# One line for all transfers in a planner, and the next pair's transposes between the halves of a pair

## Chip, cores and metric

One Trainium2 chip, one core. The metric is the device time of one execution in microseconds, taken as the median of several runs. A profiled execution, from which the rows come, has its own time.

## What is computed

The reference is an attention block with normalised queries and keys, followed by a bilinear feed-forward block (FFN). Batch 8, 12 heads, 448 positions, head dimension 64; the FFN has 3584 tokens, model width 768 and inner width 1536. All is float32; the weights come as float64.

```python
q_n, k_n = (rmsnorm(q, g_q), rmsnorm(k, g_k))
scores = scale * np.matmul(q_n, k_n.transpose(0, 1, 3, 2))
scores = scores - np.max(scores, axis=-1, keepdims=True)
attn = np.exp(scores)
attn = attn / (np.sum(attn, axis=-1, keepdims=True) + 1e-09)
attn_out = np.matmul(attn, v)
x = attn_out.transpose(0, 2, 1, 3).reshape(B * S, H * D)
out = (x @ w_a) * (x @ w_b) @ w_out
```

## The kernel before

**Pairs.** Attention is done for two heads at a time: 48 pairs, six to a batch, two heads side by side on 128 partitions. For pair `p`, `loads` (L408) brings q, k and v on SP's queue into two buffers each. `normalize` (L423) squares q and k on ScalarE (L435), sums on VectorE (L442), scales the sums (L449), takes the power -0.5 on GpSimd (L453, tile `ms`), and multiplies q by it on VectorE (L457, tile `qn`); the factor of k goes into the exponential. `transposes` (L467) turns k and q on TensorE (L486, tile `pt`), and ScalarE copies both into `qkT` (L491, L493). Keys are handled in four chunks `c`: `scores` (L499) makes `sc` on TensorE (L506) and takes the exponentials on ScalarE (L512, tile `ET`, four buffers); `values` (L518) multiplies them with v into `o` (L527); the sums over keys `su` come from matmuls with ones (L562), for pairs 0 to 11 directly from `ET`, later from `sum`, which VectorE (L540) and GpSimd (L542) add up first. `sums_over_keys` then copies `su` to a tile `rec` (L581), spreads one row of it over 112 partitions by a transfer (`few<-rec`, L587), takes the reciprocal on VectorE (L598), writes it to DRAM (`inv<-few`, L591) and brings it back over all partitions (`rec<-inv`, L595). `put_out` (L609) copies `o` into a tile `x` (L620) and multiplies by `rec` (L624). Every sixth pair (`p % 12 == 11`) instead takes the reciprocal of `su` in place (L572).

**Halves.** A pair has two halves on TensorE: chain `A{p}` holds the scores of chunks 0 and 1 and the values of chunks 2 and 3 of the pair before; chain `B{p}` the scores of chunks 2 and 3, the sums, and the values of chunks 0 and 1. `sc` has two buffers, and from pair 12 on (`LEAD`) the transposes use one of them. Scores use half of the array's rows, values and sums half of its columns, transposes and FFN products all of it (`mode`).

**Weights and FFN.** The FFN of two batches at a time (`beta` 0 to 3) is done by a scheme with seven products in place of eight, for which 18 tiles of weight factors `st` are made: `factors` (L342) loads 1.5 MB of float64 words on ScalarE's queue (L364 for w_out, L367 for w_a and w_b, tiles `hraw` and `lraw`), rounds them to float32 in seven steps (L268 on ScalarE, L269 to L277 on VectorE), forms differences (L377), and writes the result to DRAM (`kept`, L385 and L388), from where later rounds read it (`stream`, L391). `GATES` says after which pair's scores a factor may begin, `seq` in which order they are made. `quarter_products` (L763) multiplies x with the factors (`pq`, L779, 21 matmuls for each of 12 factors, in groups of three), `last_product` (L668) multiplies the result with the factors of w_out (`po`, L707).

**The order.** Nothing of this is issued where it is written. Each step is an `op` with an engine, an expected time in us, a `key`, the tiles that it reads and writes, and, for transfers, kilobytes (`kb`). `Plan.run` (L70) plays the program through with these figures: of the steps of an engine that could start now it takes the one with the lowest key, and the order that comes out is the order in which each engine is given its instructions. An engine then works strictly in that order: a step whose input is late holds up all behind it. Transfers on SP's and ScalarE's queues share eight semaphore lanes; an issue also waits until the last transfer on its lane has landed. The expected landing of a transfer (L143 to L147) is kept for SP and ScalarE apart: 250 KB per us, or 200 while the other is at work, and 2.5 us on top. At the start, 12 times four matmuls (`WARM`, L868) that compute nothing keep TensorE busy. Keys are counted in pairs: a load has `p - 2`, normalisation `p - 4`, the way of the reciprocals `p - 3`.

Of the kernel before, what the change touches and what calls it, by code (L numbers as in the profile page):

```python
# [9 lines left out]
FP32 = mybir.dt.float32  # L10
# [15 lines left out]
class Plan:  # L26
# [10 lines left out]
    LANES = 8  # L37
    LAG = 0.1
# [31 lines left out]
    def run(self):  # L70
# [18 lines left out]
        opened, free, modes, cands, dma, port = {}, {}, {}, {}, {"SP": 0.0, "ACT": 0.0}, 0.0  # L89
# [21 lines left out]
        while any(cands.values()):  # L111
# [20 lines left out]
            for x in members(n):  # L132
# [35 lines left out]
def kernel(  # L168
# [40 lines left out]
    NJ = 4  # L209
# [86 lines left out]
    def fast_body(ld, wk, ps_s, ps_o, ps_mm, dram):  # L296
# [4 lines left out]
        WARM = 12  # L301
# [40 lines left out]
        def factors(n, key, early, after):  # L342
# [16 lines left out]
            for part in range(2):  # L359
# [9 lines left out]
                op("ACT", 0.45, key - 2.5, load, after, [f"{row}/{part}"], kb=768)  # L369
# [38 lines left out]
        def loads(p, nm):  # L408
# [12 lines left out]
            op("SP", 0.5 if nm != "k" else 0.9, p - (1.8 if nm == "v" else 2.0), emit, [], [t], new=[t], kb=230)  # L421

        def normalize(p):  # L423

            ms, key = tile_of(f"ms{p}", "ms", 3), p - NORM
            for s, nm in enumerate("qk"):
                sq = tile_of(f"sq{nm}{p}", "sq", 1)

                def square(nm=nm):
# [4 lines left out]
                    if p < LEAD or SQUARE == "ACT":  # L434
                        nc.scalar.activation(t, flat, AF.Square)  # L435
                    else:
                        two[SQUARE].tensor_tensor(t, flat, flat, ALU.mult)

                def reduce(nm=nm, s=s):
                    if s == 0:  # L440
                        rs[p] = wk.tile([SP, 2, 2 * NJ], FP32, tag="ms", name="ms", bufs=3)
                    nc.vector.tensor_reduce(rs[p][:, s], xs["sq", nm, p], AX, ALU.add)  # L442
                e = "ACT" if p < LEAD else SQUARE
                op(e, {"ACT": 0.65, "POOL": 1.05, "DVE": 0.7}[e], key, square, [f"{nm}{p}"], [sq], new=[sq], lock=e != "ACT")
                op("DVE", 0.69, key, reduce, [sq], [ms], new=[ms] if s == 0 else [])

            def mean():
                msf = rs[p].rearrange("p s n -> p (s n)")
                nc.vector.tensor_scalar(msf, msf, 1.0 / D, 1e-6, ALU.mult, ALU.add)  # L449

            def root():
                msf = rs[p].rearrange("p s n -> p (s n)")
                nc.gpsimd.tensor_tensor(msf, msf, expo, ALU.pow)  # L453
# [8 lines left out]
            op("DVE", 0.18, key, mean, [], [ms])  # L462
            op("POOL", 2.95, key, root, [], [ms])
            qn = tile_of(f"qn{p}", "qn", 1)
            op("DVE", 0.7, key, apply, [ms, f"q{p}"], [qn], new=[qn], lock=True)

        def transposes(p):  # L467
            qkT = tile_of(f"qkT{p}", "qkT", 2)
            key = p - 0.5 if p < LEAD else p
            for n, nm in ((1, "k"), (0, "q")):  # L470
# [23 lines left out]
                after = [] if p < LEAD else [f"scored{p - 1}"]  # L494
# [4 lines left out]
        def scores(p, c, chain):  # L499
# [14 lines left out]
            op("PE", 0.76, p, product, [f"qkT{p}/0", f"qkT{p}/1"], [sc] + ([f"scored{p}"] if c == NJ - 1 else []), new=[sc],  # L514
               mode="rows", chain=chain)
            op("ACT", 1.12, p, exps, [sc, f"ms{p}"], [E], new=[E])
# [30 lines left out]

        def sums_over_keys(p, cs, chain):
# [19 lines left out]
            if p % (2 * HP) == 2 * HP - 1:  # L568
# [28 lines left out]
            op("SP", 0.8, p - 3.0, spread_out, [t], [few], new=[few], kb=20, dmas=2)  # L597
# [455 lines left out]
```

## Time and profile before

| | us |
|---|---|
| median of three runs | 1647.89 |
| lowest and highest run | 1640.82, 1650.4 |
| profiled execution, own time | 1654.08 |
| its span | 1652.2 |
| TensorE busy | 1604.7 |
| VectorE, ScalarE, GpSimd busy | 729.3, 432.7, 401.8 |

The span runs from the first to the last instruction, and 1.9 us of the execution lie around it. A row of the timeline gives start, duration, engine, line, operation, output and input, and in brackets the idle time before it with what ended it; matmuls of one group stand together (x8), and a float32 matmul of the program shows as two records. Ends of matmuls are modelled, so the distance between starts is the safer measure.

### The profile page before, as it was taken

How to read it: one execution, taken by the hardware profiler on the slowest of the kernel's cores; microseconds unless marked ns; L12 is line 12 of the kernel's file. 1: busy time of each engine (PE TensorE's matmuls, PEld its weight loads, DVE VectorE, ACT ScalarE, POOL GpSimd, SP SyncE). 2: the span in 40 equal slices, each digit the busy share in tenths (PEclk: the TensorE clock that was granted, in tenths of full speed). 3: DMA queues.
4: the chain of work that ended last, by engine and by line, in shares of the span. 5: the costliest groups of instructions: out<-in, count | busy, mean ns of one | idle time of the engine just before them, and what ended most of it. 6: DMA issues, size and time to landing. Idle time of an engine off the chain costs nothing.

```text
span 1652.2 us, 15068 instructions
## 1 busy us (share of the span) xinstructions
PE 1604.7 (97%) x5546; PEld 786.7 (48%) x5546; DVE 729.3 (44%) x992; ACT 432.7 (26%) x777; POOL 401.8 (24%) x200
## 2 busy tenths in 40 slices
PE   7888799999999999999999999999999999999998
PEld 5333344455444455555444455555544555555554
DVE  4776657789567532222267541122235422222331
ACT  4666563311355610000255620000034000000000
POOL 3232354211366620100265630000133000100000
PEclk9999999999999999999999999999999999999999
DMA  5676325354433443212232333322222332222121
GB/s 183 229 228 219 122 68 183 100 209 149 147 97 99 117 141 123 100 67 100 80 97 85 107 104 129 109 71 96 96 68 81 110 134 100 96 71 91 70 103 50
DMA packets 131656, 191.21 MB, mean 116 GB/s; under 512 B 62196, under 2 KB 120308, under 8 KB 121844
## 3 DMA queue, kind: packets, MB, share of 16 engines
q1 hardware_dynamic: 103828, 137.06, 25.8%
q10 hardware_dynamic: 27744, 53.09, 8.9%
q8 instruction: 46, 0.75, 0.2%
q14 instruction: 38, 0.31, 0.1%
HBM read 154.01 MB, written 35.94 MB: 115 GB/s over the span
## 4 chain that ended last, share of the span: by engine, by line
PE 83%; DMA 7%; DVE 6%; issue 1%; ACT 1%; POOL 1%; SPq 1%; ACTq 0%; DVEq 0%; POOLq 0%
PE pq L779 43%; PE po L707 23%; PE sc L506 6%; PE o L527 6%; DMA inv<-few 2%; PE su L562 2%; DMA few<-rec 2%; PE pt L486 2%; DMA rec<-inv 1%; DVE x L643 1%; DMA k_sb<-in_k_dram 1%; DVE st L377 1%; POOL ms L453 1%; DVE st L277 1%; DVE su L572 1%
## 5 line engine op out<-in xcount | busy, mean ns | idle before, releaser
L779 PE MATMUL pq<-x,st 128*128 128x448 f32 x2016 | 768.3, 542 | 3.2 <-DVE t L836 3.2
L779 PEld LDWEIGHTS pq<-x,st 128*128 128x128 f32 x2016 | 381.9, 191 | 378.7 <-issue 368.3
L512 ACT ACTIVATE ET<-sc,ms 112x448 f32<-112x448 f32 x384 | 216.2, 637 | 128.4 <-PE sc L506 117.5
L707 PE MATMUL po<-st,hT 128*128 128x384 f32 x744 | 247.3, 488 | 0.0
L542 POOL TENSOR_TENSOR sum<-sum,ET 112x896 f32<-112x896 f32 x72 | 162.2, 2253 | 197.9 <-DVE sum L540 180.1
L453 POOL TENSOR_TENSOR ms<-ms,expo 112x16 f32<-112x16 f32 x48 | 152.6, 3180 | 214.7 <-DVE ms L449 203.5
L506 PE MATMUL sc<-qkT 64*112 64x448 f32 x768 | 175.1, 573 | 26.2 <-ACT ET L512 14.1
L827 POOL TENSOR_TENSOR hT<-hT,t 128x448 f32<-128x448 f32 x24 | 27.9, 1164 | 676.4 <-DVE t L825 676.4
L707 PEld LDWEIGHTS po<-st,hT 128*128 128x128 f32 x744 | 139.4, 190 | 102.2 <-issue 9.5
L527 PE MATMUL o<-ET,v_sb 112*64 112x448 f32 x768 | 168.1, 560 | 1.0 <-ACT x L620 1.0
L707 PE MATMUL po<-st,fin 128*128 128x384 f32 x432 | 145.1, 489 | 0.0
L801 ACT COPY hT<-pq 128x448 f32<-128x448 f32 x24 | 12.8, 532 | 447.0 <-PE pq L779 447.0
L506 PEld LDWEIGHTS sc<-qkT 64*112 64x112 f32 x768 | 61.2, 175 | 120.0 <-issue 79.0
L707 PEld LDWEIGHTS po<-st,fin 128*128 128x128 f32 x432 | 80.6, 190 | 59.3 <-issue 7.0
L527 PEld LDWEIGHTS o<-ET,v_sb 112*64 112x64 f32 x768 | 51.1, 140 | 106.9 <-issue 101.5
L442 DVE TENSOR_REDUCE ms<-sq 112x8 f32<-112x512 f32 x96 | 65.1, 678 | 73.5 <-ACT sq L435 69.7
L727 DVE TENSOR_TENSOR o_sb<-fin,po 128x384 f32<-128x384 f32 x56 | 31.0, 554 | 149.9 <-PE po L707 146.2
L457 DVE TENSOR_TENSOR qn<-q_sb,ms 112x512 f32<-112x512 f32 x48 | 62.6, 1304 | 22.2 <-POOL ms L453 11.2
L839 POOL TENSOR_TENSOR hT<-hT,t 128x448 f32<-128x448 f32 x48 | 58.9, 1229 | 46.7 <-DVE t L836 46.7
L804 ACT COPY t<-pq 128x448 f32<-128x448 f32 x24 | 12.8, 533 | 187.2 <-PE pq L779 187.2
L832 DVE TENSOR_TENSOR hT<-U,pq 128x448 f32<-128x448 f32 x48 | 29.8, 621 | 68.2 <-PE pq L779 68.2
L836 DVE TENSOR_TENSOR t<-U,pq 128x448 f32<-128x448 f32 x48 | 29.6, 620 | 65.0 <-PE pq L779 63.9
(70 smaller groups left out, 980.8 us busy)
## 6 DMA issues: line engine op xcount, KB each, us to landing
st<-kept SPq DMA_DIRECT2D x36, 1344.0 KB
st<-kept_o SPq DMA_DIRECT2D x28, 1152.0 KB
kept<-st ACTq DMA_DIRECT2D x12, 1344.0 KB
q_sb<-in_q_dram SPq DMA_DIRECT2D x48, 224.0 KB
k_sb<-in_k_dram SPq DMA_DIRECT2D x48, 224.0 KB
v_sb<-in_v_dram SPq DMA_DIRECT2D x48, 224.0 KB
rec<-inv SPq DMA_DIRECT2D x88, 112.0 KB
kept_o<-st ACTq DMA_DIRECT2D x6, 1344.0 KB
```

The lines of the kernel that those rows point to most:

```text
L442: nc.vector.tensor_reduce(rs[p][:, s], xs["sq", nm, p], AX, ALU.add)
L453: nc.gpsimd.tensor_tensor(msf, msf, expo, ALU.pow)
L457: nc.vector.tensor_tensor(qns[p].rearrange("p j h d -> p h j d"), xs["q", p].rearrange("p h (j d) -> p h j d", d=D), rs[p][:, 0].rearrange ...
L486: nc.tensor.transpose(t[:, j * SP:(j + 1) * SP], x[:, j].rearrange("p h d -> p (h d)"), ident[0:SP, 0:SP])
L506: nc.tensor.matmul(t[:, e, 0:S], lhsT=qkTs[p][rows, 1, c * SP:(c + 1) * SP], rhs=qkTs[p][rows, 0, :], start=True, stop=True)
L512: nc.scalar.activation(E[:, e], scs[p, c][:, e, 0:S], AF.Exp, scale=rs[p][:, 1, 2 * c + e:2 * c + e + 1])
L527: nc.tensor.matmul(os_[p][e * D:(e + 1) * D, :], lhsT=xs["v", p][:, e, c * D:(c + 1) * D], rhs=ETs[p, c][:, e], start=(c == 0), stop=(c == ...
L542: two[ADD_UP].tensor_tensor(sums[p], sums[p], ETs[p, c], ALU.add)
L562: nc.tensor.matmul(sus[p][e * D:(e + 1) * D, :], lhsT=ones, rhs=x[:, e], start=(first and n == 0), stop=(last and n == len(parts) - 1))
L707: nc.tensor.matmul(held["po"][:, 0:HALF], lhsT=a[0]()[:, c], rhs=sts[beta, 12 + place_of[f]][:, c], start=(c == 0), stop=(c == MH - 1))
L779: nc.tensor.matmul(banks[bank][:, 0:S], lhsT=sts[at][:, f, c * P:(c + 1) * P], rhs=quads[x][:, c], start=(start and c == 0), stop=(stop an ...
L839: lambda i=i, n=n, nm=nm: two[TIMES].tensor_tensor(C(i, n), C(i, n), held[nm], ALU.mult), [t], [hp[i]],
```

## The change

All of it is in what the planner is told; the operations stay the same, but for two things named below.

- Transfers run on one line in the planner, at 300 KB per us with 2.5 us on top, whichever queue issues them; a k load counts as 400 KB.
- q and k loads get the key `p - 2.5`, v `p - 2.3`; the steps of the reciprocals' way go from `p - 3` to `p`.
- From pair 12 on the transposes of pair `p` get the key `p - 1.5` and wait for chunk 1 of pair `p - 1` (`half`) instead of chunk 3 (`scored`), so that they come between that pair's halves.
- The first two factors wait for k of pair 0; the gates of the others lie mostly earlier, five instead of eight use `hraw`, and their order is another one. `WARM` goes from 12 to 4.
- In the first four pairs q and k have their own scaling step and root (two instructions of 8 columns each for one of 16); `ms` is tracked in two parts, one for q and one for k.
- The FFN products name x and not also T3 and T4 as inputs.

```diff
+    RATE, LANDING = 300.0, 2.5
...
-                    dma[e] = max(dma[e], t) + ops[x][7] / (200.0 if dma["SP" if e == "ACT" else "ACT"] > t else 250.0)
-                    end[x] = dma[e] + 2.5
+                    dma = max(dma, t) + ops[x][7] / self.RATE
+                    end[x] = dma + self.LANDING
                     sent += [end[x]] * ops[x][11]
-                    if e == "SP":
-                        dma["ACT"] = max(dma["ACT"], t) + ops[x][7] / 300.0
...
-        WARM = 12
+        WARM = 4
+        APART = 4
...
-                op("ACT", 0.45, key - 2.5, load, after, [f"{row}/{part}"], kb=768)
+                op("ACT", 0.45, key - 1.5, load, after, [f"{row}/{part}"], kb=768)
...
-            op("SP", 0.5 if nm != "k" else 0.9, p - (1.8 if nm == "v" else 2.0), emit, [], [t], new=[t], kb=230)
+            op("SP", 0.5 if nm != "k" else 0.9, p - (2.3 if nm == "v" else 2.5), emit, [], [t], new=[t], kb=230 if nm != "k" else 400)
...
+            def roots(a, b, names):
+                msf = lambda: rs[p][:, a:b].rearrange("p s n -> p (s n)")
+                op("DVE", 0.18, key, lambda: nc.vector.tensor_scalar(msf(), msf(), 1.0 / D, 1e-6, ALU.mult, ALU.add), [], names)
+                op("POOL", 1.7 if b - a == 1 else 2.95, key,
+                   lambda: nc.gpsimd.tensor_tensor(msf(), msf(), expo[:, 0:2 * NJ * (b - a)], ALU.pow), [], names)
...
+            sums(0, "q")
+            if p < APART:
+                roots(0, 1, [f"{ms}/q"])
+            sums(1, "k")
+            if p < APART:
+                roots(1, 2, [f"{ms}/k"])
+            else:
+                roots(0, 2, [f"{ms}/q", f"{ms}/k"])
...
-            key = p - 0.5 if p < LEAD else p
+            key = p - 0.5 if p < LEAD else p - 1.5
...
-                after = [] if p < LEAD else [f"scored{p - 1}"]
+                after = [] if p < LEAD else [f"half{p - 1}"]
...
-            op("SP", 0.8, p - 3.0, spread_out, [t], [few], new=[few], kb=20, dmas=2)
+            op("SP", 0.8, p - 0.0, spread_out, [t], [few], new=[few], kb=20, dmas=2)
...
-                op("PE", KH * S / 595, key, emit, [f"{st}/{(0, 0, 0, 0, 4, 5, 6)[f]}", *parts(x), *parts(T3), *parts(T4)], [nm, "ffn"], new=[nm] if start else [], mode="full")
+                op("PE", KH * S / 595, key, emit, [f"{st}/{(0, 0, 0, 0, 4, 5, 6)[f]}", *parts(x)], [nm, "ffn"], new=[nm] if start else [], mode="full")
...
-        GATES = [0, 0, 1, 2, 3, 5, 7, 9, 10] + [12] * 9
-        seq = [12, 13, 14, 15, 16, 0, 1, 2, 3, 4, 5, 6, 7, 17, 8, 9, 10, 11]
+        GATES = [0, 0, 1, 1, 1, 2, 2, 2, 2, 2, 3, 5, 6, 6, 8, 8, 9, 10]
+        seq = [13, 12, 16, 14, 15, 0, 1, 2, 3, 4, 5, 6, 7, 8, 9, 10, 17, 11]
...
-                    factors(n, x * 1.1 + 0.5, x < 8, [f"scored{p - 1}"] if p else [])
+                    factors(n, x * 1.1 + 1.5, x < 5, [f"scored{p - 1}"] if p else ["k0"])
```

What this moves, at three places. First ScalarE at the start of the program (DMA rows are weight loads; `sq` are the squares of pairs 0 and 1, `qkT` the copies of the transposes), before:

```order
L231 ACTIVATE grow_63<-const-float32-0.0 1x256
L364 DMA hraw_90<-in_moe_w_out_dram 128x1536 x4
L435 ACTIVATE sq_128<-q_sb_96 112x512
L435 ACTIVATE sq_140<-k_sb_103 112x512
L863 COPY gain_60<-pg_147 128x1
L491 COPY qkT_188<-pt_178 128x448
L435 ACTIVATE sq_190<-q_sb_160 112x512
L493 ACTIVATE qkT_188<-pt_183,gain_60 128x448
L268 ACTIVATE st_93<-hraw_90 128x1536
L435 ACTIVATE sq_204<-k_sb_162 112x512
L512 ACTIVATE ET_207<-sc_198,ms_134 112x448 x2
```

and after:

```order
L230 ACTIVATE grow_63<-const-float32-0.0 1x256
L440 ACTIVATE sq_127<-q_sb_99 112x512
L440 ACTIVATE sq_133<-k_sb_105 112x512
L364 DMA hraw_90<-in_moe_w_out_dram 128x1536 x2
L867 COPY gain_60<-pg_141 128x1
L364 DMA hraw_90<-in_moe_w_out_dram 128x1536
L440 ACTIVATE sq_149<-q_sb_123 112x512
L364 DMA hraw_90<-in_moe_w_out_dram 128x1536
L492 COPY qkT_167<-pt_155 128x448
L440 ACTIVATE sq_170<-k_sb_125 112x512
L494 ACTIVATE qkT_167<-pt_160,gain_60 128x448
```

The two squares of pair 0 have moved ahead of all weight loads; pair 1's k square (the row with k_sb_125) now stands between the two copies of pair 0.

Then SP's queue in the pairs before pair 12 (`few`, `inv` and `rec` are the three legs of the reciprocals' way), before:

```order
L587 DMA few_468<-rec_432 56x1x8 x2
L591 DMA inv1_499<-few_468 112x8
L419 DMA v_sb_524<-in_v_dram 112x2x256
L595 DMA rec_432<-inv1_499 64x448 x2
L587 DMA few_549<-rec_520 56x1x8 x2
L416 DMA k_sb_565<-in_k_dram 112x8x64
L591 DMA inv2_591<-few_549 112x8
L419 DMA v_sb_594<-in_v_dram 112x2x256
L419 DMA q_sb_599<-in_q_dram 112x2x256
L416 DMA k_sb_612<-in_k_dram 112x8x64
L595 DMA rec_520<-inv2_591 64x448 x2
L587 DMA few_623<-rec_619 56x1x8 x2
```

and after:

```order
L591 DMA few_410<-rec_385 56x1x8 x2
L419 DMA q_sb_448<-in_q_dram 112x2x256
L595 DMA inv1_452<-few_410 112x8
L419 DMA v_sb_461<-in_v_dram 112x2x256
L416 DMA k_sb_482<-in_k_dram 112x8x64
L591 DMA few_488<-rec_484 56x1x8 x2
L419 DMA q_sb_519<-in_q_dram 112x2x256
L599 DMA rec_385<-inv1_452 64x448 x2
L595 DMA inv2_551<-few_488 112x8
L419 DMA v_sb_556<-in_v_dram 112x2x256
L416 DMA k_sb_580<-in_k_dram 112x8x64
L591 DMA few_600<-rec_577 56x1x8 x2
```

Before, `inv<-few` comes right behind the `few<-rec` that it needs, or behind one k load; after, a q load, and in the second pair also the return of the pair before, stand between the two. The loads of a pair keep the order q, v, k from pair to pair.

Last TensorE in the dense part from pair 12 on, where FFN products (`pq`) fill in, before:

```order
L506 MATMUL sc<-qkT 112x448 x4
L562 MATMUL su<-sum,ones 64x448 x2
L527 MATMUL o<-ET,v_sb 64x448 x4
L486 MATMUL pt<-ident,k_sb 128x112 x4
L486 MATMUL pt<-ident,qn 128x112 x4
L779 MATMUL pq<-x,st 128x448 x3
L506 MATMUL sc<-qkT 112x448 x4
L527 MATMUL o<-ET,v_sb 64x448 x4
L779 MATMUL pq<-x,st 128x448 x3
```

and after:

```order
L507 MATMUL sc<-qkT 112x448 x4
L566 MATMUL su<-sum,ones 64x448 x2
L528 MATMUL o<-ET,v_sb 64x448 x4
L507 MATMUL sc<-qkT 112x448 x4
L528 MATMUL o<-ET,v_sb 64x448 x4
L487 MATMUL pt<-ident,k_sb 128x112 x4
L487 MATMUL pt<-ident,qn 128x112 x4
L783 MATMUL pq<-x,st 128x448 x3
```

Before, the second half of a pair (with `su`) is followed by the transposes of the next, then FFN products, then that pair's first half, then FFN products. After, a second half is followed at once by the first half of the next pair, and transposes and one group of FFN products come behind that.

More of the change, by code (lines that the diff above doesn't have):

```diff
@@ L88, in run @@
         ready = {n: 0.0 for n in need}
-        opened, free, modes, cands, dma, port = {}, {}, {}, {}, {"SP": 0.0, "ACT": 0.0}, 0.0
+        opened, free, modes, cands, dma, port = {}, {}, {}, {}, 0.0, 0.0
         for n, k in need.items():
@@ L433, in square @@
                             x.rearrange("p j h d -> p (j h) d"))
[L434 to L453, printed above, removed]
+                    nc.scalar.activation(t, flat, AF.Square)
+                op("ACT", 0.65, key, square, [f"{nm}{p}"], [sq], new=[sq])
+                op("DVE", 0.69, key, lambda: nc.vector.tensor_reduce(rs[p][:, s], xs["sq", nm, p], AX, ALU.add), [sq], [f"{ms}/{nm}"])
+            def roots(a, b, names):
[3 more added lines that the diff above has]
+                   lambda: nc.gpsimd.tensor_tensor(msf(), msf(), expo[:, 0:2 * NJ * (b - a)], ALU.pow), [], names)
             def apply():
```

31 lines of the change are left out of this document (17 added, 14 removed).

## The prediction

> **What bounds the kernel now.** I read the page's head first, then the busy times by stage, then who waits for whom on TensorE, then the timelines of the stages where it waits.
>
> ```profile
> span 1652.2 us, 15068 instructions
> PE 1604.7 (97%) x5546; PEld 786.7 (48%) x5546; DVE 729.3 (44%) x992; ACT 432.7 (26%) x777; POOL 401.8 (24%) x200
> ```
>
> The busy times of each engine in four stages (busy us and instructions, then granted clock, DMA share, GB/s):
>
> ```profile
> 0.00:19.50 19.50, 15.97 (x98) 15.80 (x99) 2.84 (x8) 3.12 (x5) 3.76 (x9) 0.82 0.71 245
> 19.50:195.00 175.50, 148.01 (x726) 55.79 (x726) 125.16 (x169) 110.80 (x195) 52.20 (x16) 0.94 0.63 201
> 195.00:320.00 125.00, 119.74 (x443) 52.04 (x438) 83.00 (x104) 56.70 (x99) 55.73 (x26) 0.98 0.38 120
> 320.00:1644.00 1324.00, 1320.51 (x4285) 663.11 (x4284) 517.78 (x712) 262.04 (x480) 290.07 (x151) 1.00 0.31 103
> ```
>
> TensorE is the bound, and nearly all that it loses lies ahead of 320 us. The first 19.5 us hold only warm-up matmuls. From 19.5 to 195 us (pairs 0 to 12 and the first eight weight factors) it is idle for 175.5 - 148.0 = 27.5 us, and a clock of 0.94 takes 0.06 x 175.5 = 10.5 us more: 38 us. From 195 to 320 us the loss is 5.3 idle plus 0.02 x 125 = 2.5, together 8 us. Behind that it is 3.5 us in 1324. Whom TensorE waits for there (us in total, times, longest), first over the whole run, then what the engines behind it wait for between 20 and 196 us:
>
> ```profile
> PE sc L506 <- ACT ET L512: 14.1, 8, 3.5
> PE sc L506 <- ACT qkT L493: 12.0, 5, 5.2
> PE su L562 <- DVE x L624: 3.5, 2, 2.2
> ...
> DVE few L598 <- DMA few<-rec: 20.4, 5, 6.8
> ACT sq L435 <- DMA k_sb<-in_k_dram: 8.4, 2, 5.4
> ACT sq L435 <- DMA q_sb<-in_q_dram: 6.3, 2, 4.9
> ACT ET L512 <- DMA few<-rec: 4.7, 1, 4.7
> ```
>
> The scores wait for ScalarE (its exponentials and its copies of the transposed q), and ScalarE and VectorE stand in their own queues behind transfers that land later than the order allowed for. The small transfers in the chain of waits show by how much:
>
> ```profile
> 58.82 8.27 DMA few<-rec
> ...
> 145.21 2.24 DMA few<-rec
> ```
>
> The same kind of transfer takes 2.2 us at one time and 8.3 at another. When such a wait reaches TensorE it is paid twice, for the clock falls (a group of eight score matmuls at 66.95 us against one at 74.63):
>
> ```profile
> 66.95 3.33 PE L506 MATMUL sc<-qkT 64*112 64x448 f32 x8 [3.50 <-ACT ET L512]
> ...
> 74.63 1.76 PE L506 MATMUL sc<-qkT 64*112 64x448 f32 x8
> ```
>
> **The change part by part.** *The start.* The timeline of the first pair:
>
> ```profile
> 8.93 0.82 ACTq L364 DMA_DIRECT2D hraw<-in_moe_w_out_dram  x2
> 9.80 0.63 ACT L435 ACTIVATE sq<-q_sb 112x512 f32<-112x512 f32 x1 [7.35 <-DMA k_sb<-in_k_dram]
> ...
> 11.84 0.69 DVE L442 TENSOR_REDUCE ms<-sq 112x8 f32<-112x512 f32 x1
> ...
> 12.03 7.66 PE L868 MATMUL warm<-ident 128*128 128x128 f32 x40
> ...
> 12.89 2.92 POOL L453 TENSOR_TENSOR ms<-ms,expo 112x16 f32<-112x16 f32 x1 [11.44 <-DVE ms L449]
> 15.85 0.69 DVE L457 TENSOR_TENSOR qn<-q_sb,ms 112x512 f32<-112x512 f32 x1 [3.11 <-POOL ms L453]
> ...
> 21.07 0.63 ACT L493 ACTIVATE qkT<-pt,gain 128x448 f32<-128x448 f32 x1
> ...
> 21.75 1.76 PE L506 MATMUL sc<-qkT 64*112 64x448 f32 x8 [1.29 <-ACT qkT L493]
> ```
>
> ScalarE issues weight loads ahead of its first square and stands until 8.93 for a lane that k's load holds; then a warm-up of 7.66 us holds the transposes until 19.5, though q is ready at 16.5. The change puts both squares ahead of the weight loads, which start only when k has landed, takes the root of q alone, and cuts the warm-up from 48 matmuls to 16. How soon a q or k load lands with nothing beside it is bounded by two rows that come later:
>
> ```profile
> 527.30 0.34 SPq L419 DMA_DIRECT2D q_sb<-in_q_dram  x1
> ...
> 530.04 0.63 ACT L435 ACTIVATE sq<-q_sb 112x512 f32<-112x512 f32 x1 [3.19 <-DMA q_sb<-in_q_dram]
> ```
>
> ScalarE waited for that q and got it 2.7 us after its issue. Issued at 0.74, q is there at 3.5; square 0.63, sum 0.69 and mean 0.17 (an estimate with the gaps: 5.1); the root is half as wide, and no row shows one: it costs between half of 2.92 and all of it, so 1.5 to 2.9, and I take 2.2. With 0.69 for the product q is normalised at 8 to 8.8. The order of ScalarE then puts pair 1's k square between the two copies of pair 0, so that the first scores come at 11 rather than 21.75: 10.75 us. Of that I take 1.75 off for the clock, since after a pause it stood at half for six slices (the busy times of the first and last of them):
>
> ```profile
> 12.00:13.00 1.00, 1.00 (x5) 0.98 (x6) 0.70 (x2) 0.16 (x1) 0.10 (x1) 0.50 1.00 418
> ...
> 17.00:18.00 1.00, 1.00 (x7) 1.00 (x7) 0.00 (x0) 0.00 (x0) 0.00 (x0) 0.50 0.23 49
> ```
>
> Six us at half speed are 3 us of lost work; the first pair's matmuls wait for ScalarE's exponentials anyway, so half to two thirds of it counts. **Start: -9**, between -5 (k lands as late as 7) and -11. The Trainium skill ("TensorE: Matmul & The Clock Gate", section "What's actually happening") has the full clock return after one window of about 3.4 us of sustained work; by that the loss is at most 1.7 and the start an estimated -10, and the six slices here say longer.
>
> *The order under one line for all transfers, loads ahead of returns, factors spread otherwise.* The planner now counts every transfer on one line of 300 KB per us, so it expects small transfers late when weights move; the returns of 1/sum lose their urgency (key p - 3 becomes p) and q, k and v gain half a pair. The number of instructions does not change. What it can win is the 38 us of stage two. What it cannot do: in that stage TensorE works 148 us at a clock of 0.94, 138 at full clock, and VectorE's 125 and ScalarE's 111 stay below that, but the eight factors still lie there. If the stage shrinks by 19 us, VectorE is at 125 / 156 = 80% and served in strict order. So not all the waits go: waits of 20.4 + 8.4 + 6.3 + 4.7 = 40 us on landings stand behind it, and the change addresses each kind, but none by a buffer. I take half. **Stage two: -19**, between -34 and +5 (the same bytes in less time land later). SP's queue carries more loads ahead of the returns; a return that lands later holds its VectorE product and its `rec` tile (three of them, so three pairs of slack), not TensorE. **195 to 320: -3**, a little under half of the 8, between -7 and +4, since factors 9 to 18 still have to be made there, one for each 21 FFN products. That these products no longer name T3 and T4 among their inputs lets three of them start before pair 11 is done; they do the same work, and I cost it at nothing.
>
> *The transposes of the next pair between the halves.* One pair of the dense part on TensorE, with a group of FFN matmuls (`pq`) after each half:
>
> ```profile
> 448.18 1.76 PE L506 MATMUL sc<-qkT 64*112 64x448 f32 x8
> 449.87 0.97 PE L562 MATMUL su<-sum,ones 112*64 112x448 f32 x4
> 450.67 1.67 PE L527 MATMUL o<-ET,v_sb 112*64 112x448 f32 x8
> 452.28 0.60 PE L486 MATMUL pt<-ident,k_sb 112*128 112x112 f32 x4
> ...
> 453.10 2.43 PE L779 MATMUL pq<-x,st 128*128 128x448 f32 x6
> 455.46 1.76 PE L506 MATMUL sc<-qkT 64*112 64x448 f32 x8
> ...
> 458.81 2.52 PE L779 MATMUL pq<-x,st 128*128 128x448 f32 x6
> 461.26 1.76 PE L506 MATMUL sc<-qkT 64*112 64x448 f32 x8
> ...
> 632.69 178.31 PE L779 MATMUL pq<-x,st 128*128 128x448 f32 x474
> ```
>
> In the long run a matmul takes 178.3 / 474 = 0.376 us, so six take 2.26. The group behind `o` takes 461.26 - 458.81 = 2.45: 0.19 for going to the full array and back. By the order 36 such groups stand behind `o` before and 6 after; those behind the transposes stay 34. The matmuls themselves move into other groups. 30 x 0.19 = 5.7; **-5.5** with the few new changes of form. Against this, a half now follows the last one at once. From the start of one half: scores 1.69, sums 0.80, values 1.61, so the next scores start at 4.10. ScalarE's exponentials:
>
> ```profile
> 540.44 1.76 PE L506 MATMUL sc<-qkT 64*112 64x448 f32 x8
> 541.56 2.21 ACT L512 ACTIVATE ET<-sc,ms 112x448 f32<-112x448 f32 x4 [1.78 <-PE sc L506]
> ```
>
> They start 1.12 behind the scores and take 2.21: the buffers are free at 3.33, 0.8 us ahead of need. The second half ends at 7.40, the transposes (453.10 - 452.28) at 8.22, and with the FFN group of 455.46 - 453.10 = 2.36 the next pair starts at 10.6 us instead of 461.26 - 448.18 = 13.1. The transposes now wait for the first half's scores and sit in one of the two score buffers; behind them on TensorE stand the FFN group and the second half. ScalarE's two copies of them (at most 0.63 each, the row of L493 above) end near 9.5, over 0.8 us ahead of the second half at 10.6. So the cover is there, but thin where 1.3 MB of FFN weights share SP's queue with a k load; **+5** for new waits, between 0 and +20.
>
> Sum against the profiled execution's own 1654.1 us (span 1652.2 and 1.9 around it): -9 - 19 - 3 - 5.5 + 5 = -31.5, so 1622.6. The median of the runs shown, 1647.89, lies 6.2 below that execution; for the median I say 1617.
>
> **The rivals.** *Nearly every wait goes.* If the order fits the transfers, stage two falls to 138 us: -10 - 36 - 7 - 5.5 + 0 = -58.5, so 1595.6, 1589 as a median. For it: the waits are all on landings. Against: queues in strict order at 80%.
>
> *The factors set the pace.* If the eight factors (VectorE's 125 us with waits in between) and not the pairs decide when the FFN begins, the early start only becomes waiting: -5.5 - 3 = -8.5, 1645.6, as a median 1639.5, no change that can be told. Against: VectorE is at 71% there now.
>
> *The line is no line.* The late small transfers may not be late because of weights, and then a planner that reckons so gains only the q and k waits, 8.4 + 6.3, about half of which reach TensorE: -9 - 7 - 3 - 5.5 + 5 = -19.5, 1634.6, as a median 1628. The rows of 2.24 and 8.27 speak for the line; the Trainium skill ("DMA: Bandwidth & Descriptors", section "Queues, rings and completion order") says that each DMA engine takes turns between queues packet by packet, so a short transfer of SP's would not stand behind a whole weight load of ScalarE's. An 8.3 us transfer of 1.8 KB agrees badly with that.
>
> *Slower: the halves run dry.* Without FFN matmuls between the halves, scores wait for ScalarE in every pair of the dense part. The place is the first scores of a half, the slack 0.8 us; each us beyond it costs 31 pairs x 1 = 31 us, so ScalarE has to be 1.8 us late per pair to eat the whole gain. At 2.3 late it is -31.5 + 46 = +15, 1669, as a median 1662. Against: per pair ScalarE has exponentials of 2 x 2.21, two squares and two copies of 0.63 at most, and two more copies of that size: 4.4 + 6 x 0.63 = 8.2 us, which fit into 10.6.
>
> **How the numbers follow.** The forecast has 0.50, nearly every wait gone 0.15, the line that is none 0.12, the factors' pace 0.14, dry halves 0.07, and 0.02 that the order gains nothing at all. About 0.5% (8 us) is what a measurement of this kernel can tell from no change. The first three and a third of the fourth are faster by more: 0.81; the rest of the fourth and the last are the same: 0.12; slower 0.07. The range leaves out half of the second case below and the slower case above: 1594 to 1641.
>
> **What would show it.** Right: first scores at 10 to 12 us; pair 12's scores done some 28 us earlier, and a clock above 0.96 up to there; ScalarE's waits on q and k and VectorE's on `few` at half or less; no group of FFN matmuls between halves and pairs of 10.3 to 10.6 us with scores that wait for nobody. Wrong: score waits on ScalarE of over 1 us in each dense pair; an FFN start that waits for `st`; a stage two as long as now.

## The result, and the profile after

| | before | after |
|---|---|---|
| median, us | 1647.54 (4 runs, 1640.82 to 1650.4) | 1601.39 (4 runs, 1600.07 to 1603.11) |
| ratio, 95% interval | | 0.9726 (0.9695 to 0.9757) |
| profiled execution, its span | 1654.08, 1652.2 | 1601.34, 1599.5 |

The change makes the kernel 2.7% faster. The forecast was 1617 us with a range from 1594 to 1641: the sign and the range hold, and the gain is 46 us instead of 31. The head of the profile after, and the same stages as before (busy us and instructions of TensorE, its weight loads, VectorE, ScalarE and GpSimd, then granted clock, DMA share and GB/s):

```profile
span 1599.5 us, 14956 instructions
PE 1579.5 (99%) x5482; PEld 779.8 (49%) x5482; DVE 728.5 (46%) x996; ACT 435.3 (27%) x777; POOL 398.6 (25%) x204
```

```profile
0.00:19.50 19.50, 16.18 (x84) 10.48 (x86) 6.19 (x16) 12.86 (x21) 8.39 (x13) 0.91 0.90 283
19.50:195.00 175.50, 167.36 (x834) 65.83 (x832) 141.57 (x194) 126.15 (x225) 74.03 (x26) 0.97 0.68 213
195.00:320.00 125.00, 124.43 (x405) 59.55 (x402) 99.64 (x114) 39.19 (x62) 38.35 (x20) 1.00 0.44 148
```

From 19.5 to 195 us TensorE is now idle for 175.5 - 167.4 = 8.1 us, and the clock costs 0.03 x 175.5 = 5.3: 13.4 us against 38 before. VectorE and ScalarE do more in the same stretch (141.6 against 125.2, 126.2 against 110.8) and yet hold TensorE less. From 195 to 320 us 0.6 us is left of 8. What TensorE waits for longest in the whole run (us in total, times, longest), then what stands behind it between 20 and 196 us:

```profile
PE sc L507 <- ACT qkT L494: 8.0, 5, 4.3
PE pt L487 <- ACT ET L513: 2.1, 1, 2.1
```

```profile
ACT sq L440 <- DMA k_sb<-in_k_dram: 5.3, 1, 5.3
DVE x L628 <- DMA rec<-inv: 2.5, 2, 2.2
DVE few L602 <- DMA few<-rec: 2.2, 3, 1.3
...
ACT sq L440 <- DMA q_sb<-in_q_dram: 0.7, 1, 0.7
```

Three of the four longest waits on landings before (20.4, 8.4 and 6.3 us) are 2.2, 5.3 and 0.7. The fourth, which the prediction's list does not show, is VectorE's wait for the returned sums. It is 2.5 us after; before it was

```profile
DVE x L624 <- DMA rec<-inv: 8.8, 3, 4.4
```

The start, in the timeline after:

```profile
5.07 3.90 POOL L448 TENSOR_TENSOR ms<-ms,expo 112x8 f32<-112x8 f32 x2 [3.63 <-DVE ms L446]
6.79 0.69 DVE L452 TENSOR_TENSOR qn<-q_sb,ms 112x512 f32<-112x512 f32 x1
...
10.09 2.09 PE L507 MATMUL sc<-qkT 64*112 64x448 f32 x8 [1.89 <-ACT qkT L494]
```

The first scores come at 10.09 instead of 21.75. One root of 8 columns takes at most 1.7 us (5.07 to 6.79). How the gain of 52.7 us between the two profiled executions is spread shows from three marks, the transposes of pairs 2, 12 and 15, before and after:

```profile
38.60 0.60 PE L486 MATMUL pt<-ident,k_sb 112*128 112x112 f32 x4
...
173.28 0.60 PE L486 MATMUL pt<-ident,k_sb 112*128 112x112 f32 x4
...
219.51 0.60 PE L486 MATMUL pt<-ident,k_sb 112*128 112x112 f32 x4
```

```profile
23.97 0.41 PE L487 MATMUL pt<-ident,k_sb 112*128 112x112 f32 x2
...
133.92 0.72 PE L487 MATMUL pt<-ident,k_sb 112*128 112x112 f32 x4 [2.06 <-ACT ET L513]
...
172.21 0.60 PE L487 MATMUL pt<-ident,k_sb 112*128 112x112 f32 x4
```

Up to pair 2 it is 38.60 - 23.97 = 14.6 us, from pair 2 to pair 12 another 134.7 - 110.0 = 24.7, from pair 12 to pair 15 another 46.2 - 38.3 = 7.9, and the other 5.4 in all the rest of the run. These plain differences flatter the early part, because the changed order has done less work at the second and third mark. At pair 12 it is half a pair (eight records each of `sc`, `o` and `su`, 1.7 + 1.6 + 1.6 = 4.9 us). At pair 15 it is a later half (1.7 + 1.6 + 0.8 = 4.1 us) and 12 records of FFN products (4.5 us), together 8.6. For the same work the four parts are 14.6, 19.8, 4.2 and 14.1 us: some three quarters of the gain lie ahead of pair 15. In the dense part the halves follow each other:

```profile
421.51 2.43 PE L783 MATMUL pq<-x,st 128*128 128x448 f32 x6
423.87 1.76 PE L507 MATMUL sc<-qkT 64*112 64x448 f32 x8
425.56 0.97 PE L566 MATMUL su<-sum,ones 112*64 112x448 f32 x4
426.37 1.67 PE L528 MATMUL o<-ET,v_sb 112*64 112x448 f32 x8
427.97 1.76 PE L507 MATMUL sc<-qkT 64*112 64x448 f32 x8
...
432.14 1.31 PE L783 MATMUL pq<-x,st 128*128 128x448 f32 x3
```

A pair takes 432.14 - 421.51 = 10.63 us as forecast, no score waits, and the new waits that I feared there are absent. One new long stop stands elsewhere, where the pairs pass into the dense part:

```profile
162.81 1.84 PE L507 MATMUL sc<-qkT 64*112 64x448 f32 x4 [4.32 <-ACT qkT L494]
```

### The profile page after: what moved, and what is told of

Same layout as the page of the kernel before. It is cut to its first block, busy times and chain, and to the rows that moved or that the text cites. A ratio compares the mean times of both kernels' runs of the same rounds, so it can differ in the third digit from the quotient of the medians.

```text
span 1599.5 us, 14956 instructions
## 1 busy us (share of the span) xinstructions
PE 1579.5 (99%) x5482; PEld 779.8 (49%) x5482; DVE 728.5 (46%) x996; ACT 435.3 (27%) x777; POOL 398.6 (25%) x204
## 4 chain that ended last, share of the span: by engine, by line
PE 90%; DVE 4%; DMA 2%; POOL 2%; issue 1%; ACT 1%; SPq 0%; ACTq 0%; POOLq 0%; DVEq 0%
PE pq L783 47%; PE po L711 24%; PE sc L507 8%; PE o L528 7%; PE su L566 2%; PE pt L487 2%; POOL ms L448 2%; DMA rec<-inv 1%; DMA inv<-few 1%; DVE ms L442 1%; DVE st L377 0%; DVE qn L452 0%; DVE st L276 0%; DVE x L647 0%; DMA few<-rec 0%
## 5 line engine op out<-in xcount | busy, mean ns | idle before, releaser
L711 PE MATMUL po<-st,hT 128*128 128x384 f32 x744 | 244.0, 487 | 0.0
L543 POOL TENSOR_TENSOR sum<-sum,ET 112x896 f32<-112x896 f32 x72 | 152.5, 2118 | 203.8 <-DVE sum L541 201.5
L448 POOL TENSOR_TENSOR ms<-ms,expo 112x16 f32<-112x16 f32 (+1 forms) x52 | 161.2, 3101 | 122.1 <-DVE ms L446 107.8
L507 PE MATMUL sc<-qkT 64*112 64x448 f32 x768 | 171.2, 564 | 8.0 <-ACT qkT L494 8.0
L528 PE MATMUL o<-ET,v_sb 112*64 112x448 f32 x768 | 164.7, 550 | 0.0
L452 DVE TENSOR_TENSOR qn<-q_sb,ms 112x512 f32<-112x512 f32 x48 | 47.8, 996 | 31.3 <-POOL ms L448 29.0
```

What stands on the lines that cost most here:

```text
L448: lambda: nc.gpsimd.tensor_tensor(msf(), msf(), expo[:, 0:2 * NJ * (b - a)], ALU.pow), [], names)
L452: nc.vector.tensor_tensor(qns[p].rearrange("p j h d -> p h j d"), xs["q", p].rearrange("p h (j d) -> p h j d", d=D), rs[p][:, 0].rearrange ...
L507: nc.tensor.matmul(t[:, e, 0:S], lhsT=qkTs[p][rows, 1, c * SP:(c + 1) * SP], rhs=qkTs[p][rows, 0, :], start=True, stop=True)
L528: nc.tensor.matmul(os_[p][e * D:(e + 1) * D, :], lhsT=xs["v", p][:, e, c * D:(c + 1) * D], rhs=ETs[p, c][:, e], start=(c == 0), stop=(c == ...
L543: two[ADD_UP].tensor_tensor(sums[p], sums[p], ETs[p, c], ALU.add)
L711: nc.tensor.matmul(held["po"][:, 0:HALF], lhsT=a[0]()[:, c], rhs=sts[beta, 12 + place_of[f]][:, c], start=(c == 0), stop=(c == MH - 1))
```

## The experiments

My theory (W): the start and the waits on late landings carry most of the gain, the place of the transposes only the 0.19 us of 30 groups. Rival (H): the halves carry it. Under W stood a second question: is it the common line that makes landings punctual (L), or the keys and gates (K)? Times are medians; each ratio is to runs of the kernel before taken beside it.

| | kernel | us | ratio, 95% interval |
|---|---|---|---|
| e1 | after, transposes back behind the pair | 1602.06 | 0.9721 (0.9707 to 0.9735) |
| e2 | before, transposes between the halves | 1629.24 | 0.9878 (0.9860 to 0.9895) |
| e3 | after, a line for each queue | 1632.29 | 0.9902 (0.9885 to 0.9920) |
| e4 | before, the common line | 1628.96 | 0.9875 (0.9858 to 0.9893) |
| e5 | after, the old warm-up and roots | 1598.10 | 0.9693 (0.9679 to 0.9708) |
| e6 | after, the old keys of loads and returns | 1618.40 | 0.9815 (0.9800 to 0.9830) |
| e7 | after, the old gates of the factors | 1607.29 | 0.9749 (0.9735 to 0.9764) |
| e8 | after, pairs 12 and 13 as in e1 | 1596.36 | 0.9690 (0.9673 to 0.9707) |
| e9 | e8, the first pause filled | 1597.86 | 0.9685 (0.9668 to 0.9702) |
| e10 | after, the old key of returns only | 1604.46 | 0.9733 (0.9714 to 0.9753) |
| e11 | after, lag 0.12 (control) | 1607.42 | 0.9755 (0.9738 to 0.9771) |
| e12 | after, the line at 600 | 1617.65 | 0.9808 (0.9791 to 0.9825) |

### e1 and e2: the halves alone

```diff
 e1, in the kernel after
-            key = p - 0.5 if p < LEAD else p - 1.5
+            key = p - 0.5 if p < LEAD else p
-                after = [] if p < LEAD else [f"half{p - 1}"]
+                after = [] if p < LEAD else [f"scored{p - 1}"]
 e2, in the kernel before: the same lines the other way
```

> The changed kernel with one part undone: the q and k transposes of pair 12 on stand behind the last scores of the pair before again (key p, waiting for scored), not between its halves. Theory W (most of the gain is waits on late landings in the first 320 us, the place of the transposes is worth only 30 groups x 0.19 us): 1607 us, that is 4 to 9 over the changed kernel, with the first scores at 10.1 us and the stretch from 19.5 to 195 us within 3 us of 175.5. Rival H (the halves following each other carry the gain, by a wait in front of each pair's scores that they hide): 1625 us or more, and waits of scores for the copies of the transposes in every dense pair.

> The kernel before with one part of the change alone: the transposes of pairs 12 on between the halves of the pair before (key p - 1.5, behind the second scores). Theory W: 1642 us, that is 3 to 9 under the kernel before, and the stretch up to 195 us as long as before to within 5 us. Rival H: 1625 us or less.

e1 came out 0.7 us over the kernel after, and e2 18.5 under the kernel before. H is out by e1, but W missed both, by 5 and by 13 us. For e2 the trace shows a part of why. The scores behind pair 12's transposes (173.28 us) before, then the same place in e2, where they stand behind transposes between the halves:

```profile
179.51 3.33 PE L506 MATMUL sc<-qkT 64*112 64x448 f32 x8 [5.24 <-ACT qkT L493]
```

```profile
166.70 1.01 PE L506 MATMUL sc<-qkT 64*112 64x448 f32 x4
169.87 1.01 PE L506 MATMUL sc<-qkT 64*112 64x448 f32 x4 [2.16 <-ACT qkT L493]
```

Between halves, the transposes have half a pair of work behind them, and ScalarE copies them meanwhile; behind the pair, where no FFN group is ready yet, TensorE stands through the copies and loses its clock too (3.33 us for eight scores where 1.76 is usual). I had counted the move as fewer changes of form alone and not as cover. This one place is worth some 5 us (5.24 - 2.16 of waiting and 1.6 of slow clock). Behind the first scores of pair 20 (442.38 us before, 425.57 in e2) another 8.7 are gained: 5.4 by the fewer FFN groups, as e8 will show, the rest because waits for VectorE of 3.5 us are gone there. The profiled executions differ by 23.3, so the other 9.6, in the early pairs, are not explained. For e1, its transposes also cost the 0.19 us per group again, but the stop of 4.3 us at 162.81 is not there. Its waits for the copies, with the longest at the end of the row:

```profile
PE sc L507 <- ACT qkT L494: 7.3, 5, 2.0
```

The changed order pays for its own gain in one place, then; that made e8.

### e3, e4 and e12: the line

```diff
 e3, in the kernel after
-                    dma = max(dma, t) + ops[x][7] / self.RATE
-                    end[x] = dma + self.LANDING
+                    dma[e] = max(dma[e], t) + ops[x][7] / self.RATE
+                    end[x] = dma[e] + self.LANDING
 e4, in the kernel before: RATE, LANDING and the lines of one line, k loads at 400
 e12, in the kernel after
-    RATE, LANDING = 300.0, 2.5
+    RATE, LANDING = 600.0, 2.5
```

> The changed kernel with one part altered: each queue is a line of its own in the planner (300 per us and 2.5 us of landing for each), instead of one line for both. TensorE's instructions stand in the same order as in the changed kernel; only those of ScalarE, VectorE and the issues differ. Theory L (the common line is what makes the planner keep the small loads and returns from landing late): 1616 us, 7 to 25 over the changed kernel, with VectorE's waits for the spread sums and ScalarE's for q and k back to half or more of the 35 us of before. Rival K (the keys of loads and returns and the gates do it, whatever the line): 1601 us, within 4.

> The kernel before with the common line alone (300 per us, 2.5 us of landing, 400 KB counted for a k load); keys, gates, start and transposes stay. Theory L: 1630 us (1622 to 1640), the gain in the stretch up to 195 us. Rival K: within 5 us of the kernel before. Third possibility, the line by itself delays factors behind loads so that groups of FFN work run dry: slower than before by over 5 us.

> The changed kernel with the common line twice as fast in the planner (600 per us for 300), the landing of 2.5 us kept. The trace moves 230 to 310 GB/s in the first slices. Theory L (what counts is that the planner's line is as slow as the transfers are): small transfers are asked for as if loads were over in half the time, 1612 us or more, with VectorE's wait for the spread sums at 8 us or more. Rival (one line in either rate keeps the order of the queues, and that is enough): 1601 us, within 4.

e3 lost 31 us, more than expected, with TensorE's list word for word that of the kernel after: all of it is in when ScalarE, VectorE and the queues do their part. Its waits between 20 and 196 us:

```profile
DVE few L602 <- DMA few<-rec: 16.9, 5, 4.7
DVE x L628 <- DMA rec<-inv: 9.1, 5, 3.0
ACT sq L440 <- DMA k_sb<-in_k_dram: 5.9, 2, 3.9
ACT sq L440 <- DMA q_sb<-in_q_dram: 3.2, 2, 2.9
```

The three kinds that theory L named were 35.1 us before and are back at 16.9 + 5.9 + 3.2 = 26.0; with the returned sums it is 35.1 of 43.9. The chain of waits has one of these transfers:

```profile
74.27 6.20 DMA few<-rec
```

What was issued ahead of it and beside it:

```profile
71.30 0.57 SPq L419 DMA_DIRECT2D v_sb<-in_v_dram  x1
71.97 0.65 SPq L416 DMA_DIRECT2D k_sb<-in_k_dram  x1
72.72 0.62 SPq L419 DMA_DIRECT2D q_sb<-in_q_dram  x1
73.40 1.64 SPq L591 DMA_DIRECT2D few<-rec  x2
73.58 0.99 ACTq L367 DMA_DIRECT2D lraw<-in_moe_w_a_dram  x2
```

The 1.8 KB stand behind three loads of 224 KB on their own queue, while two weight loads of 768 KB run on ScalarE's.

How it reaches TensorE, in e3's timeline:

```profile
80.56 0.20 DVE L602 RECIPROCAL few<-few 112x8 f32<-112x8 f32 x1 [4.75 <-DMA few<-rec]
...
81.35 0.63 ACT L440 ACTIVATE sq<-q_sb 112x512 f32<-112x512 f32 x1 [3.03 <-DVE ms L442]
...
84.44 1.09 PE L507 MATMUL sc<-qkT 64*112 64x448 f32 x2 [5.68 <-ACT ET L513]
```

VectorE stands 4.75 us at a reciprocal whose sums have not landed; behind it on VectorE waits a sum of squares that ScalarE's only `sq` buffer hangs on; ScalarE's exponentials stand behind the next square and behind the issue of a store that waits for VectorE again, and the scores stand behind them. The `x` that this reciprocal leads to is made for FFN products, and the first of these comes in e3 at 156.63 us. So a planner that expects it too early turns a transfer with slack into a stop of three engines. e4, the line alone, gained 18.8 us: VectorE's wait for `few` falls from 20.4 to 4.1, and the first scores come at 17.91. Both agree with L. e12 agrees in the time (16 us lost) and not in the way: `few` costs only 3.1 us there, and a k that lands late costs much at one place, in front of the first scores (ScalarE, then TensorE):

```profile
15.84 0.63 ACT L440 ACTIVATE sq<-k_sb 112x512 f32<-112x512 f32 x1 [4.43 <-DMA k_sb<-in_k_dram]
```

```profile
17.48 3.33 PE L507 MATMUL sc<-qkT 64*112 64x448 f32 x8 [8.19 <-ACT qkT L494]
```

At twice the rate the planner takes pair 1's k for landed and puts its square ahead of both copies that pair 0's scores need (in the kernel after it stands between them). The k lands late, and the scores start at 17.48 instead of 10.09: 7.4 of the 16 us. A line twice as fast as the transfers is too fast, then; 300 KB per us is near the 230 to 310 GB/s that the trace after moves in its first four slices, and no other rate was run.

### e6, e10 and e7: keys and gates

```diff
 e6, in the kernel after; e10 has the second line alone, for all four steps
-            op("SP", 0.5 if nm != "k" else 0.9, p - (2.3 if nm == "v" else 2.5), ...
+            op("SP", 0.5 if nm != "k" else 0.9, p - (1.8 if nm == "v" else 2.0), ...
-            op("SP", 0.8, p - 0.0, spread_out, ...
+            op("SP", 0.8, p - 3.0, spread_out, ...
 e7, in the kernel after
-        GATES = [0, 0, 1, 1, 1, 2, 2, 2, 2, 2, 3, 5, 6, 6, 8, 8, 9, 10]
-        seq = [13, 12, 16, 14, 15, 0, 1, 2, 3, 4, 5, 6, 7, 8, 9, 10, 17, 11]
+        GATES = [0, 0, 1, 2, 3, 5, 7, 9, 10] + [12] * 9
+        seq = [12, 13, 14, 15, 16, 0, 1, 2, 3, 4, 5, 6, 7, 17, 8, 9, 10, 11]
```

> The changed kernel with one part undone: the keys of loads and returns as before (q, k at p - 2.0, v at p - 1.8, the four steps of a return at p - 3.0). The common line stays. The first experiments put VectorE's wait for the spread sums at 20.4 us before, 16.9 with queues of their own, 2.2 to 4.1 with the common line. Theory L (the line does it, the keys little): 1604 us, 0 to 6 over the changed kernel, VectorE's wait for the spread sums under 6 us. Rival K (the returns' key p - 3.0 puts a return before loads that are due, so that q and k are late): 1612 us or more, with ScalarE's waits for q and k at 10 us or more.

> The changed kernel with half of the sixth experiment: only the four steps of a return have their key of before (p - 3.0), loads keep theirs. That experiment cost 17 us. Theory R (the returns' key does it: asked for ahead of loads that are due, they stand on SP's queue and wait there for VectorE while loads wait behind): 1612 us or more, with ScalarE waiting for q or k 8 us or more. Rival Q (the key of q, k and v does it, asked for half a pair later): within 5 of the changed kernel.

> The changed kernel with one part undone: the table of which factors are asked for behind which pair, and the order of the factors, as before (8 of them early instead of 5). Theory W: the common line places whatever comes, so 1606 us, 0 to 10 over the changed kernel, the difference in the stretch from 19.5 to 195 us. Rival T (the table was made for the line and is worth as much as it): 1615 us or more.

e6 lost 17 us, where L had at most 6, and e10 only 3: R falls. So the key of q, k and v is what counts, alone or together with that of the returns; loads alone with their old key were not run. Two stops stand out in e6 (124.14 us behind a k that landed late, 184.19 where an FFN group waits for VectorE):

```profile
124.14 3.33 PE L507 MATMUL sc<-qkT 64*112 64x448 f32 x8 [7.38 <-ACT qkT L494]
...
184.19 3.35 PE L783 MATMUL pq<-x,st 128*128 128x448 f32 x4 [7.40 <-DVE x L647]
```

e7 lost 6 us, as W had it; but see e11.

### e5 and e9: the start

```diff
 e5, in the kernel after
-        WARM = 4
-        APART = 4
+        WARM = 12
+        APART = 0
 e9, in e8's transposes
+                    [nc.tensor.matmul(warms[0][:, 0:P], lhsT=ident, rhs=ident, start=True, stop=True) for x in range(7 if p == n == 0 else 0)]
```

> The changed kernel with the start undone where the planner lets it be: 12 warming steps instead of 4, and the roots of q and k of the first four pairs taken together again (APART = 0). The factors still wait for k of pair 0. Theory W: the first scores come later than 10.1 us by one root of 16 against 8 columns (2.9 against 1.7 us, with a k square and reduce ahead of it) and by eight more warming steps, so at 13 to 17 us; 1606 us, 3 to 8 over the changed kernel, since the start is a path with no cover. Rival G (the gate of the factors made the start, not these two): within 2 of the changed kernel.

> The kernel of the experiment that left pairs 12 and 13 behind the last scores, with seven more warming products on TensorE between the transposes and the first scores of pair 0, where it waits 2.3 us for ScalarE; every other instruction stands where it stood. In that kernel the granted clock is 0.91 over the first 19.5 us and the transposes at 12 to 14 us take 1.0 us where 0.6 is usual. Theory C (the pause of 2.3 us loses the clock): first scores at 10.4 us as there, transposes at 12 us near 0.6 us, granted clock 0.97 or more over the first 19.5 us, and 1.5 to 3 us less in all: 1594 us. Rival: the clock goes for another reason, times as there, 1596 us; or the seven products delay the scores by over 1 us and it is 1597 us.

In e5 the first scores come at 17.11 and pair 2's transposes at 29.65, 5.7 us behind the kernel after: that part is near what W had, and it shows that warm-up and roots carry 5.7 of the 14.6 us up to pair 2. Yet the whole is 3.3 us faster than the kernel after, where W had 3 to 8 slower and G within 2: the order that came out behind it has no stop as long as the 4.3 us at 162.81 (the longest wait of TensorE from 20 to 196 us is 2.0). e9 looks at the clock. A pause in front of the first scores, by slices of 1 us of e8 (granted clock is the third number from the end):

```profile
11.00:12.00 1.00, 1.00 (x8) 0.26 (x4) 0.66 (x1) 0.45 (x1) 1.00 (x1) 0.87 0.95 379
12.00:13.00 1.00, 1.00 (x5) 0.55 (x4) 0.00 (x0) 1.00 (x3) 0.54 (x1) 0.50 1.03 417
...
15.00:16.00 1.00, 1.00 (x8) 0.43 (x4) 0.00 (x0) 0.32 (x1) 0.00 (x0) 0.92 1.05 396
```

The clock is at half for 0.26 + 3 + 0.16 = 3.4 us, and with the pause filled (e9) it stays at 1.00: transposes at 12.10 take 0.60, and pair 2's come at 22.87 instead of 24.32, 1.45 us earlier. But the trace of e1, where the same pause stands unfilled, keeps the clock as well:

```profile
10.21 1.76 PE L507 MATMUL sc<-qkT 64*112 64x448 f32 x8 [1.97 <-ACT qkT L494]
11.90 0.60 PE L487 MATMUL pt<-ident,k_sb 112*128 112x112 f32 x4
```

In front of the first scores, pauses of 1.89 (after), 2.04 (e10), 2.12 (e7) and 2.33 us (e8) lost the clock; 1.97 (e1), 1.98 (e11) and 2.15 us (e3) did not. So what the loss costs is measured (1.45 us here, 1.44 at pair 2 between the kernel after and e1), but one execution of e9 does not show that the filling saved it. In e9 the gain is gone at 41 us:

```profile
41.53 2.13 PE L507 MATMUL sc<-qkT 64*112 64x448 f32 x8 [2.24 <-ACT qkT L494]
```

In e8 these scores started at 41.10 with a wait of 0.34. TensorE had come earlier and ScalarE had not; so it stopped, lost the clock and was 2.1 us behind by the next pair. The total is that of e8 within its spread: C is wrong on the time, and on the clock it agrees with e9 without being shown.

### e8 and e11: the order's own accidents

```diff
 e8, in the kernel after
-            key = p - 0.5 if p < LEAD else p - 1.5
+            key = p - 0.5 if p < LEAD else p if p < 14 else p - 1.5
-                after = [] if p < LEAD else [f"half{p - 1}"]
+                after = [] if p < LEAD else [f"scored{p - 1}"] if p < 14 else [f"half{p - 1}"]
 e11, in the kernel after
-    LAG = 0.1
+    LAG = 0.12
```

> The changed kernel with the transposes of pairs 12 and 13 alone put back behind the last scores of the pair before; from pair 14 on they stay between the halves. The changed kernel's one long stop (scores at 162.81 us, 4.3 us for the copies of the transposes) comes from pair 15's q and k, and the first experiment, without any transposes between halves, did not have it and lost the 0.19 us of 30 groups. Theory S (that stop is an accident of the order around pairs 12 to 15, and the 0.19 us per group is real): 1597 us, 3 to 6 under the changed kernel. Rival: the stop stays or another takes its place, 1601 us, within 2.

> A control: the changed kernel with a number of the planner that stands for no part of the change (the lag from one engine to another, 0.1 to 0.12 us). The order of the early part changes with it (216 lines of difference on TensorE's list against 112 in the half undone keys). Theory A (the order of the first 320 us comes out by accident within some 5 to 10 us, whatever is set): a time that differs from the changed kernel by 2 to 10 us, either way. Rival: within 2 us, so that differences of 4 us and more between these kernels are the edit's own.

e8 is the fastest median of all, with no stop at 157 to 163 us; its runs (1594.61 to 1599.51) and those of the kernel after (1600.07 to 1603.11) do not overlap. Against e1, from which it differs in the transposes from pair 14 on, it is 1602.06 - 1596.36 = 5.7 us faster: the size of 30 x 0.19. The control moved the time by 6.0 us with nothing in it that should, so the total alone would not prove it. The trace shows the place. From the first scores of pair 20 on, in e1 and in e8:

```profile
391.75 1.76 PE L507 MATMUL sc<-qkT 64*112 64x448 f32 x8
```

```profile
391.02 1.76 PE L507 MATMUL sc<-qkT 64*112 64x448 f32 x8
```

To the end of its span e1 takes 1599.1 - 391.75 = 1207.4 us and e8 1594.1 - 391.02 = 1203.1, though e8 has six more records of FFN products ahead of it (2.3 us). For the same work that is 6.6 us; one wait for VectorE in e1 is 1.2 of it. The other 5.4 belong to FFN groups behind `o`, of which 29 follow in e1 and 4 in e8: about 0.2 each. The kernel after, e2 and the control take 1203.1 to 1203.4 us from the same place, so what the control moved lies ahead of pair 20. So among these kernels a difference of up to some 6 us may be the luck of an order, and e5's -3, e7's +6 and e10's +3 prove nothing for or against the line that was edited, unless the trace shows the place. The losses of e3, e6 and e12 (31, 17 and 16 us) are well beyond it, as far as one control can tell.

## Why the prediction was right, and where its sum was off

- **Start (-9).** The mechanism is right, the size too small: first scores at 10.09 (I had 11), 11.7 us gained, and 14.6 up to pair 2, since a stop in front of pair 1 went as well. A clock above 0.96 was forecast up to pair 12; it was 0.91 in the first 19.5 us and 0.97 behind. The 1.75 us taken off for the clock were fair (1.44 between the kernel after and e1). By the Trainium skill ("TensorE: Matmul & The Clock Gate", section "What's actually happening") the clock is judged in windows of about 3.4 us; I held the six slices of before against that, and e8's 3.4 us agree with it.
- **Stage two (-19).** This is the term that was mis-sized. The step was "So not all the waits go: waits of 20.4 + 8.4 + 6.3 + 4.7 = 40 us on landings stand behind it, and the change addresses each kind, but none by a buffer. I take half." Of those 40 us 8.2 are left (2.2 + 5.3 + 0.7; the fourth is gone): four fifths went, and the stage lost 38 - 13.4 = 24.6 us of idle time and slow clock. (The sum left out the 8.8 us for the returned sums, of which 2.5 are left; and 148 us at a clock of 0.94 are 139 at full clock, not 138, which changes nothing.) A buffer was not needed, as the comparison with e3 shows: with the same buffers and the same list on TensorE, a planner that knows when transfers land removes the waits by asking for their result later. My reason against it, VectorE at 80% in strict order, was right in the number (141.57 / 175.5 = 81%) and no obstacle.
- **195 to 320 us (-3).** It gave 8 - 0.6 = 7.4, past the end of my range. The e2 trace shows a cause that I had not priced: transposes between halves are covered by the second half where FFN groups are still scarce. It is not the only one, since in e1, without it, TensorE is busy for all of these 125 us at a clock of 1.00.
- **The transposes (-5.5).** Right, by 10.63 us per pair and by the 5.4 us behind pair 20 in e8 against e1. Its gain is hidden in the plain comparison e1, because the changed order brought the stop at 162.81 us.
- **New waits (+5).** None in the dense part; the cover of 0.8 us per half held. The one new stop is at pair 15, ahead of the dense part.
- **The rivals.** "The line is no line" is refuted by e3 and e12. By the Trainium skill ("DMA: Bandwidth & Descriptors", section "Queues, rings and completion order") each DMA engine takes turns between queues packet by packet. I held the 8.27 us of a 1.8 KB transfer against that, and this was a misreading: as in e3, that transfer stood behind v, k and q loads of its own queue (issued at 53.61, 54.28 and 57.24 us), with weight loads beside them (55.88 and 56.25). That agrees with turns as well as with one line, and no run here separates the two. The pace of the factors and the dry halves did not come. "Nearly every wait goes" (1589) was nearer than the forecast: 12 us below the result, where 1617 is 16 above. And 6.2 us of the forecast were taken off because the profiled execution of the kernel before lay above its median. That of the kernel after does not (1601.34 against 1601.39), so the parts add up to 52.7 us between the profiled executions, where the medians differ by 46.

The parts do not add up. The line alone is worth 18.8 us on the kernel before (e4) and the halves alone 18.5 (e2), while without the line the change keeps 15 us (e3) and without the halves all of its 46 (e1): so the two overlap. The stop of 5.24 us at pair 12 is an example: e2 shortens it, and without the halves e1 does not have it either (its longest wait of that kind is 2.0). What each of the gates and of the first pair's new order of loads is worth by itself was not measured.

## What to carry to other kernels

In queues of strict order, ask for a result when it will have landed, and price all transfers on one line at the rate that the trace moves: an instruction that waits for a small transfer too early stops what stands behind it, on three engines in a row. Work that has slack belongs behind what has none, and a step that another engine must finish belongs ahead of work that covers it. Before a gain of a few microseconds is put down to an edit of a planner, vary a number that means nothing and see how far the time moves by itself.

## What was not expected of the hardware

- A pause of 1.89 us on TensorE was followed by some 3.4 us at half clock in the kernel after (10.09 us), while after one of 1.97 us at the same place in e1 the clock stayed at 1.00, and after one of 2.16 us in e2 four scores took their usual 1.01 us (169.87 us); the length of a pause alone does not tell.
- A root of 16 columns on GpSimd took 2.91 us at 170.05 us in the kernel after and 4.25 us at 46.32 us in e8; one of 8 columns 1.64 us at 31.11 us in e8.
